# Two token blocks take turns in the first stage, with one order of loads and zero products in the gaps, in an attention kernel with two feed-forward layers

## The chip, the cores and the metric

The kernel runs on one core of one Trainium2 chip. The metric is the device time of one execution in microseconds (us). The median of three runs stands for a kernel.

## The reference: what is computed

Everything is float32, except the weights, which come as float64. First an attention in chunks of 32 queries, each of which sees its own 32 keys, 16 to the left, 8 to the right and 8 memory keys. Its output, 3072 tokens by 512, goes through two feed-forward layers of the same shape, one behind the other.

```python
        scores = scale * np.matmul(q_c, k_full.transpose(0, 1, 3, 2))
        scores = scores - np.max(scores, axis=-1, keepdims=True)
        a = np.exp(scores)
        a = a / (np.sum(a, axis=-1, keepdims=True) + 1e-09)
        out[:, :, c_start:c_end] = np.matmul(a, v_full)
...
    x = np.ascontiguousarray(attn_out.transpose(0, 2, 1, 3)).reshape(B * S, H * D)
...
    h = x @ w_in                                   # first layer, 512 -> 2048
    g = h * (1.0 / (1.0 + np.exp(-1.702 * h)))
    return (g @ w_out).astype(np.float32)          # 2048 -> 512
...
    h = x @ w_in                                   # second layer
    g = np.maximum(h, 0.0) + alpha * np.minimum(h, 0.0)
    return (g @ w_out).astype(np.float32)
```

## The kernel before

**Blocks and steps.** Each layer runs over six blocks of 512 tokens, and each block over 16 slices f of the hidden width, 128 columns each. A step is one block and one slice: `mm1` makes h in 12 products of 128x512 (TensorE; input and weight are each split into a high and a low part, and high-high, low-high and high-low are kept), `act1` and `split_g` make g and its two parts (ScalarE: tanh, cast; VectorE: two passes), and `mm2_t` adds 12 products into four accumulators y, which stay in four PSUM banks for the 16 steps of a block. The y products of a step are written behind the h products of the next (`LAG = 1`). After the 16th, `finish1` scales the four banks into SBUF, alternately on ScalarE and VectorE, and writes them to the DRAM tensor y1, which the second layer reads.

**Weights.** Piece s holds slice s of w_in and of w_out, 1 MB of float64 (`w_load`, two DMAs). It is turned into a high and a low float32 part: an absolute value on ScalarE (`w_abs`), four passes on VectorE (`w_bits`, L102 to L109), a cast on ScalarE (`w_high`, L120) and one more pass on VectorE (`w_low`, L125). The 16 pieces of the first layer are prepared while block 0 runs, since its step f needs piece f. `w_tick` hands out the next piece; the main loop asks for piece `W0 + WN*f/4`.

**Attention.** A group m is 128 tokens: scores (`a_scores`, tile sc), maximum and subtraction on VectorE, exp on ScalarE, sum and scaling on VectorE (into aspr or atpr), transposes on TensorE (pt) and copies on ScalarE (p), values (`a_pv`, tile xp), and a split into the high (ScalarE, L270) and low part (VectorE, L271) of x. A block needs four groups. Groups 0 to 3 run ahead of the first step (`NSTART = 4`), with two buffers for each of q, k and v (`SB = 2`); groups 4 to 7 run during block 0, and so on.

**Order.** A scheduler orders each engine's instructions at build time, except where `tc.keep_in_program_order` pins one; on the chip each engine goes through its list as it stands. All loads and stores are issued from one DMA queue on SyncE (SP), in order: an issue that waits for a free buffer holds the ones behind it.

Of the kernel before, what the change touches and what calls it, by code (L numbers as in the profile page):

```python
# [33 lines left out]
LAG = 1  # L34
NSTART = 4
WTICKS = (2, 3)
WAHEAD = 2
LEAD = 4
OPB = 3
W0 = 3  # L40
WN = 5
SB = 2
NWB = 4
NWARM = 28
# [4 lines left out]
@with_exitstack  # L49
def fused_kernel(ctx: ExitStack, tc: tile.TileContext, qs, ks, vs, ident, w_in1, w_out1, w_in2, w_out2, alpha, out):  # L50
    nc = tc.nc
# [78 lines left out]
    def w_tick(limit):  # L130
        s = wtick[0]
        if s >= limit + 1:
            return False
        if s - 1 in wst:
            w_low(s - 1)
        while wloaded[0] < limit and wloaded[0] <= s + (WAHEAD if wloaded[0] < BOOST else 1):
            w_load(wloaded[0])
            wloaded[0] += 1
        if s < limit:
            w_abs(s)  # L140
            w_bits(s)
# [59 lines left out]
    def a_max(m):  # L201
# [8 lines left out]
        mx = ap["pool"].tile([128, 2 * HP], F32, tag="mx", name=f"mx{m}")  # L210
        ex = ap["pool"].tile([128, 2 * HP, KW], F32, tag="p0", name=f"ex{m}", bufs=ap["pb"])
# [32 lines left out]
    def a_pcopy(m, g):  # L244
        s = st[m]
        s["p", g] = ap["pool"].tile([NK, HP, 128], F32, tag=f"p{g}", name=f"p{m}_{g}", bufs=ap["pb"] if g == 0 else None)
        nc.scalar.copy(s["p", g], s["pt", g])
# [88 lines left out]

    def mm2_t(p, y, gs, n, f):
        gh, gl = gs
        wh, wl = wt[p, f]
        for m in range(NKC):  # L340
            for i, (w, g) in enumerate(((wh, gh), (wh, gl), (wl, gh))):
                nc.tensor.matmul(  # L342
                    y[m][:, :n], w[:, 1, m * 128:(m + 1) * 128], g[:, :n],
                    start=(f == 0 and i == 0), stop=(f == NF - 1 and i == 2),
                )
# [10 lines left out]

    def finish1(y, t0, n):
# [32 lines left out]

    steps = []
    t0 = 0
    for j, n in enumerate(P1_BLOCKS):
        steps += [(1, j, t0, n, f) for f in range(NF)]
        t0 += n
    t0 = 0
    for j, n in enumerate(P2_BLOCKS):
        steps += [(2, j, t0, n, f) for f in range(NF)]
        t0 += n
    n1 = len(P1_BLOCKS)  # L400
    need = [done_tick(int(p1_start[j + 1]) // SQ - 1) for j in range(n1)]
    last1 = (n1 - 1) * NF

# [5 lines left out]

    t = ps2.tile([128, 128], F32, tag="h", name="warm")  # L410
    for i in range(NWARM):
        nc.tensor.matmul(t, warm, warm, start=True, stop=True)

    att_open("as", SB, 2)
# [6 lines left out]
    stags = ("a0", "a1", "y2", "y3")  # L421
    a_scores(0, stags[0])
    a_max(0)
    a_exp(0)
    for t in range(NSTART + 1):
        if t + 1 < NSTART:
            a_scores(t + 1, stags[(t + 1) % 4])
            a_load_v(t + 1)
        if t + 2 < NSTART:
            a_load(t + 2)  # L430
        if t < NSTART:
            a_norm(t)
            for g in range(2):
                a_trans(t, g, "h")
                a_pcopy(t, g)
        if t + 1 < NSTART:
            a_max(t + 1)
            a_exp(t + 1)
        if t < NSTART:
            a_pv(t, f"y{t % 2}")  # L440
            a_xcopy(t)
        if t in WTICKS:
            w_tick(NPC)
        if t == 1:
            nc.sync.dma_start(out=al_sb, in_=alpha.rearrange("(f p) -> p f", p=128))

    att.close()
    side["wpb"] = ctx.enter_context(tc.tile_pool(name="wpb", bufs=NWB))
    att_open("at", 1, 1)
    a_load(NSTART)  # L450
    a_load_v(NSTART)

    def do_mm2(i):
        p, j, t0, n, f = steps[i]
        if f == 0:
            ys[p, j] = [ps1.tile([128, DM], F32, tag=f"y{m}", name=f"y{m}") for m in range(NKC if p == 1 else n // 128)]
        (mm2_t if p == 1 else mm2_n)(p, ys[p, j], pend.pop(i), n, f)
        if f == NF - 1:
            (finish1 if p == 1 else finish2)(ys.pop((p, j)), t0, n)

    def attend(j, h):
        goal = need[j] + (need[j + 1] - need[j]) * min(1, h / (2 * NF - LEAD))
        while tick[0] < goal:
            a_tick()

    for i, (p, j, t0, n, f) in enumerate(steps):
        if i < NF:
            while wtick[0] < min(NPC + 1, W0 + (WN * f) // 4):
                w_tick(NPC)
        if i == last1:  # L470
            att.close()
# [6 lines left out]
        if i < last1:  # L478
            attend(j, 2 * f + 1)
        pend[i] = split_g(g, n, nc.vector)  # L480
        if i >= LAG:
            do_mm2(i - LAG)
        if i < last1:
            attend(j, 2 * f + 2)

# [56 lines left out]
```

## Time and profile before

| | |
|---|---|
| median of three runs | 1182.05 us (1181.15 to 1183.36) |
| the profiled execution | 1184.33 us, of which the span is 1182.6 us |
| TensorE (PE) busy | 1150.4 us, 97% of the span |
| VectorE (DVE) busy | 611.1 us, 52%; in 50 to 150 us it is 94.30 of 100 us |
| ScalarE (ACT) busy | 321.5 us, 27% |
| first h product | at 41.53 us |
| first block done (last y products) | about 160.9 us |
| second block done | about 262.4 us |

The shares are means over very different stages. In the first 160 us VectorE and the loads work much harder than later, and TensorE has its only gaps there; behind them TensorE is busy throughout. A matmul's end is modelled in the profile and overlaps the next, so the pitch from start to start is what it costs.

### The profile page before, as it was taken

To read this page: it belongs to the slowest core of one execution; us is meant where nothing else is said; L and a number is where in the kernel's file an instruction comes from. 1 tells how busy PE (TensorE), PEld (TensorE's weight loads), DVE (VectorE), ACT (ScalarE), POOL (GpSimd) and SP (SyncE) were. 2 spreads that over 40 slices of the span, in tenths; PEclk is the share of its full clock that TensorE was granted. 3 is DMA by queue.
4 is the path that set the end of the run, shared out by engine and by line. 5 is a ranking of instruction groups with operands and counts; after the bars stand their busy time and mean duration, and the time that the engine had idled before them with its cause. 6 is when DMAs were issued, how large, how long until landed. Compare 5 with 4: busy or idle time off the path is not lost.

```text
span 1182.6 us, 14925 instructions
## 1 busy us (share of the span) xinstructions
PE 1150.4 (97%) x6364; PEld 942.3 (80%) x6364; DVE 611.1 (52%) x871; ACT 321.5 (27%) x479; POOL 2.4 (0%) x10
## 2 busy tenths in 40 slices
PE   5799999999999999999999999999999999999998
PEld 5577788888888888888888788888888888888886
DVE  5899934343343434343699874434434434344433
ACT  2555433232323223223456321111111111111111
POOL 0000000000000000000000000000000000000000
PEclk8799999999999999999999999999999999999999
DMA  6964313121121212112544500200100000000000
GB/s 211 275 220 155 133 69 94 47 75 55 50 91 60 70 48 83 48 62 71 191 166 145 189 23 1 72 1 5 67 1 1 36 1 1 36 1 8 29 1 36
DMA packets 43578, 86.49 MB, mean 73 GB/s; under 512 B 5048, under 2 KB 21560, under 8 KB 43512
## 3 DMA queue, kind: packets, MB, share of 16 engines
q1 hardware_dynamic: 43512, 85.54, 21.9%
q8 instruction: 50, 0.82, 0.3%
q14 instruction: 16, 0.13, 0.0%
HBM read 72.95 MB, written 12.58 MB: 72 GB/s over the span
## 4 chain that ended last, share of the span: by engine, by line
PE 90%; DVE 4%; DMA 4%; ACT 1%; issue 1%; SPq 0%; ACTq 0%
PE h L312 42%; PE y L352 21%; PE y L342 21%; DMA wraw<-w_out 2%; PE xp L256 2%; PE sc L195 2%; PE pt L242 2%; DMA k<-ks 1%; DVE wtmp L109 1%; DVE wtmp L106 1%; DVE wlo L125 1%; DVE wtmp L102 0%; ACT wtmp L96 0%; DVE gl L334 0%; DVE atpr L232 0%
## 5 line engine op out<-in xcount | busy, mean ns | idle before, releaser
L312 PE MATMUL h<-x,whi 128*128 128x512 f32 x768 | 244.6, 398 | 2.7 <-ACT whi L120 1.9
L312 PE MATMUL h<-yx,whi 128*128 128x512 f32 x768 | 239.1, 390 | 1.1 <-DVE t L327 1.1
L333 ACT CAST gh<-t 128x512 fp32r<-128x512 f32 x192 | 119.2, 621 | 441.2 <-DVE t L327 372.5
L334 DVE TENSOR_TENSOR gl<-t,gh 128x512 fp32r<-128x512 f32 x192 | 132.4, 690 | 106.7 <-ACT gh L333 106.3
L326 DVE TENSOR_SCALAR t<-h,al_sb 128x512 f32<-128x512 f32 x96 | 72.0, 750 | 196.1 <-PE h L312 196.1
L312 PEld LDWEIGHTS h<-x,whi 128*128 128x128 f32 x768 | 143.8, 190 | 34.3 <-ACT whi L120 3.5
L312 PEld LDWEIGHTS h<-yx,whi 128*128 128x128 f32 x768 | 144.1, 188 | 32.4 <-DVE t L327 1.6
L321 DVE SCALAR_TENSOR_TENSOR t<-t,h 128x512 f32<-128x512 f32 x96 | 65.8, 685 | 184.9 <-ACT t L320 184.5
L312 PE MATMUL h<-x,wlo 128*128 128x512 f32 x384 | 152.1, 396 | 0.5 <-DVE wlo L125 0.5
L342 PE MATMUL y<-gl,whi 128*128 128x512 f32 x384 | 151.3, 394 | 0.4 <-DVE gl L334 0.4
L342 PE MATMUL y<-gh,wlo 128*128 128x512 f32 x384 | 150.7, 392 | 0.0
L312 PE MATMUL h<-yx,wlo 128*128 128x512 f32 x384 | 149.9, 390 | 0.0
L352 PE MATMUL y<-whi,gh 128*128 128x512 f32 x384 | 149.8, 390 | 0.0
L352 PE MATMUL y<-wlo,gh 128*128 128x512 f32 x384 | 149.7, 390 | 0.0
L352 PE MATMUL y<-whi,gl 128*128 128x512 f32 x384 | 142.6, 390 | 0.0
L342 PE MATMUL y<-gh,whi 128*128 128x512 f32 x384 | 128.1, 398 | 3.4 <-ACT gh L333 3.2
L320 ACT ACTIVATE t<-h 128x512 f32<-128x512 f32 x96 | 57.4, 598 | 185.5 <-PE h L312 185.4
L342 PEld LDWEIGHTS y<-gh,whi 128*128 128x128 f32 x384 | 70.7, 188 | 20.5 <-ACT gh L333 5.5
L312 PEld LDWEIGHTS h<-x,wlo 128*128 128x128 f32 x384 | 72.6, 189 | 16.7 <-DVE wlo L125 0.9
L342 PEld LDWEIGHTS y<-gl,whi 128*128 128x128 f32 x384 | 72.6, 189 | 16.3 <-DVE gl L334 0.8
L342 PEld LDWEIGHTS y<-gh,wlo 128*128 128x128 f32 x384 | 72.5, 189 | 15.6
L312 PEld LDWEIGHTS h<-yx,wlo 128*128 128x128 f32 x384 | 72.1, 188 | 15.5
(50 smaller groups left out, 916.0 us busy)
## 6 DMA issues: line engine op xcount, KB each, us to landing
wraw<-w_in SPq DMA_DIRECT2D x32, 512.0 KB
wraw<-w_out SPq DMA_DIRECT2D x32, 512.0 KB
q<-qs SPq DMA_DIRECT2D x24, 512.0 KB
k<-ks SPq DMA_DIRECT2D x24, 416.0 KB
v<-vs SPq DMA_DIRECT2D x24, 416.0 KB
y<-o SPq DMA_DIRECT2D x24, 256.0 KB
yraw<-y SPq DMA_DIRECT2D x6, 1024.0 KB
out<-o SPq DMA_DIRECT2D x24, 256.0 KB
```

Of the source, the lines that this page charges most:

```text
L106: nc.vector.scalar_tensor_tensor(out=a, in0=top, scalar=0xC0000000, in1=a, op0=ALU.bitwise_and, op1=ALU.bitwise_or)
L195: nc.tensor.matmul(sc[half[c], g, j, :], s["q"][:, g, j, c], s["k"][:, g, j, run[c]], start=True, stop=True,)
L242: nc.tensor.transpose(s["pt", g][:, j, :], s["pr"][:, g, j, :], id_sb)
L256: nc.tensor.matmul(x[half[z], g, j, :].rearrange("p (c q) -> p c q", c=2), s["v"][:, g, (2 * j + z) * D:(2 * j + z + 1) * D], p[:, j, z], ...
L312: nc.tensor.matmul(h[:, :n], w[:, 0, k * 128:(k + 1) * 128], x[:, z, k, :n], start=(i == 0), stop=(i == 3 * NKC - 1))
L320: nc.scalar.activation(out=t[:, :n], in_=h[:, :n], func=AF.Tanh, scale=1.702 / 2)
L321: nc.vector.scalar_tensor_tensor(out=t[:, :n], in0=t[:, :n], scalar=1.0, in1=h[:, :n], op0=ALU.add, op1=ALU.mult)
L326: nc.vector.tensor_scalar(out=t[:, :n], in0=h[:, :n], scalar1=0.0, scalar2=al_sb[:, f:f + 1], op0=ALU.min, op1=ALU.mult)
L333: nc.scalar.copy(gh[:, :n], g[:, :n])
L334: lo_eng.tensor_tensor(out=gl[:, :n], in0=g[:, :n], in1=gh[:, :n].bitcast(F32), op=ALU.subtract)
L342: nc.tensor.matmul(y[m][:, :n], w[:, 1, m * 128:(m + 1) * 128], g[:, :n], start=(f == 0 and i == 0), stop=(f == NF - 1 and i == 2),)
L352: nc.tensor.matmul(y[m], g[:, m * 128:(m + 1) * 128], w[:, 1, :], start=(f == 0 and i == 0), stop=(f == NF - 1 and i == 2),)
```

## The change

Blocks 0 and 1 are cut into four phases: slices 0 to 5 of block 0, the same of block 1, then slices 6 to 15 of block 0 and of block 1. The weight pieces 0 to 5 serve 12 steps before piece 6 is needed. At the end of the first two phases ScalarE writes half-finished y sums to y1 (all four banks, the DMAs issued from ScalarE's own queue), and at the end of the other two they are loaded back (`load_part`) and added by VectorE. Eight groups instead of four run in the part that is written out by hand: four ahead of the first step, four during the first four steps. Their q is stored without zeros (half the bytes), and GpSimd writes the zeros. There are five buffers for q and k and six for v. The loads alternate between groups and weight pieces; alpha goes behind the weights. The absolute value on ScalarE of pieces 1 to 6 keeps its place in the program. Products of a zero tile (128x128, bfloat16), 24 at a time and in seven places (168), stand in TensorE's list between the parts of groups 0 to 3.

```diff
@@
+NFIRST = 4
+NSTART = 8
+HEAD = 6
+PINNED = 7
+NKEEP = 24
+WTICKS = (0, 2)
...
+SB = 5
+NWB = 8
...
-        nc.scalar.activation(out=a.bitcast(F32), in_=wst[s][0][:, :, 1].bitcast(F32), func=AF.Abs)
+        i = nc.scalar.activation(out=a.bitcast(F32), in_=wst[s][0][:, :, 1].bitcast(F32), func=AF.Abs)
+        if 0 < s < PINNED:
+            tc.keep_in_program_order(i)
...
     def a_load(m):
+        if m < NSTART:
+            q = ap["pool"].tile([128, 2, 2, CHUNK, 2 * HP], F32, tag="q", name=f"q{m}")
+            for z in range(2):
+                nc.gpsimd.memset(q[half[z], :, 1 - z], 0.0)
+                nc.sync.dma_start(out=q[half[z], :, z].rearrange("p g q i -> p g (q i)"), in_=q0[m, half[z]])
...
+    def finish1(y, j, last):
+        t0, n = int(p1_start[j]), P1_BLOCKS[j]
+        if not last:
+            for m in range(NKC):
+                o = op.tile([128, TBM], F32, tag="o", name="o")
+                nc.scalar.mul(o[:, :n], y[m][:, :n], 0.5)
+                nc.scalar.dma_start(out=y1[m, :, t0:t0 + n], in_=o[:, :n])
+            return
+        part = parts.pop(j, None)
         for m in range(NKC):
             o = op.tile([128, TBM], F32, tag="o", name="o")
-            if m % 2:
+            if part is not None:
+                nc.vector.scalar_tensor_tensor(
+                    out=o[:, :n], in0=y[m][:, :n], scalar=0.5, in1=part[:, m, :n], op0=ALU.mult, op1=ALU.add
+                )
+            elif m % 2:
...
+    phases = [(0, 0, HEAD), (1, 0, HEAD), (0, HEAD, NF), (1, HEAD, NF)]
+    phases += [(j, 0, NF) for j in range(2, len(P1_BLOCKS))]
...
+    def keep_warm(n):
+        t = ps1.tile([128, 128], F32, tag="a1", name="warm")
+        for i in range(n):
+            tc.keep_in_program_order(nc.tensor.matmul(t, warm, warm, start=True, stop=True))
...
     a_load(0)
     a_load_v(0)
+    nc.sync.dma_start(out=id_sb, in_=ident)
     w_load(0)
-    nc.sync.dma_start(out=id_sb, in_=ident)
-    a_load(1)
-    wloaded[0] = 1
+    for m in range(1, NFIRST):
+        a_load(m)
+        a_load_v(m)
+    w_load(1)
...
+    for t in range(NFIRST):
+        if t + 1 < NFIRST:
+            a_scores(t + 1, stags[t + 1])
+            keep_warm(NKEEP)
+        a_norm(t)
...
+        a_load(t + NFIRST)
+        a_load_v(t + NFIRST)
+        if t < 3:
+            w_load(wloaded[0])
+            wloaded[0] += 1
...
+            while wtick[0] < min(NPC + 1, 3 + i if i < HEAD else 3 + HEAD + (3 * (i - HEAD)) // 4):
                 w_tick(NPC)
...
+        if p == 1 and f == 0 and j == 2:
+            tc.keep_in_program_order(nc.sync.dma_start(out=al_sb, in_=alpha.rearrange("(f p) -> p f", p=128)))
+        if p == 1 and f == NF - 2 and ph == 2:
+            a_load(NSTART)
+            a_load_v(NSTART)
```

The lists themselves show it at three places. The number behind a name tells tiles apart, the one behind wraw, whi and wlo is the weight piece. From the third step of block 2 on (on SyncE from group 10's q on) the lists of before and of the change are the same.

First place: SyncE's queue of DMA issues at the start, from the second group's v (before) and q (change) on. Before:

```order
L186 DMA v_184<-vs 104x1024
L445 DMA al_sb<-alpha 128x16x1
L179 DMA q_186<-qs 128x1024
L181 DMA k_188<-ks 128x832
L179 DMA q_254<-qs 128x1024
L181 DMA k_256<-ks 128x832
L186 DMA v_252<-vs 104x1024
L186 DMA v_320<-vs 104x1024
L85 DMA wraw_1_366<-w_in 128x4x256
```

And with the change:

```order
L188 DMA q_143<-q 64x2x256 x2
L191 DMA k_148<-ks 128x832
L202 DMA v_150<-vs 104x1024
L188 DMA q_152<-q 64x2x256 x2
L191 DMA k_157<-ks 128x832
L202 DMA v_159<-vs 104x1024
L188 DMA q_161<-q 64x2x256 x2
L191 DMA k_166<-ks 128x832
L202 DMA v_168<-vs 104x1024
L87 DMA wraw_1_170<-w_in 128x4x256
```

Alpha is gone from between the groups, and piece 1 stands directly behind group 3, with no wait for a buffer ahead of it.

Second place: VectorE's list around the last weight piece of the first layer (wlo_15). Before, where h_1365 is the h of the 15th step:

```order
L106 SCALAR_TENSOR_TENSOR wtmp<-wraw_15_1102,wtmp 128x1024
L334 TENSOR_TENSOR gl<-t,gh 128x512
L109 SCALAR_TENSOR_TENSOR wtmp<-wraw_15_1102,wtmp 128x1024
L271 TENSOR_TENSOR x_672<-xp_1324,x_672 128x2x4x64
L213 TENSOR_REDUCE mx_1360<-sc_1343 128x8
L125 TENSOR_TENSOR wlo_15_1211<-wtmp,whi_15_1210 128x1024
L214 TENSOR_TENSOR ex_1361<-sc_1343,mx_1360 128x512
L321 SCALAR_TENSOR_TENSOR t<-t,h_1365 128x512
```

With the change, where h_1590 and h_1632 are the h of the 16th and the 17th step:

```order
L110 SCALAR_TENSOR_TENSOR wtmp<-wraw_15_1542,wtmp 128x1024
L337 SCALAR_TENSOR_TENSOR t<-t,h_1590 128x512
L350 TENSOR_TENSOR gl<-t,gh 128x512
L113 SCALAR_TENSOR_TENSOR wtmp<-wraw_15_1542,wtmp 128x1024
L350 TENSOR_TENSOR gl<-t,gh 128x512
L337 SCALAR_TENSOR_TENSOR t<-t,h_1632 128x512
L129 TENSOR_TENSOR wlo_15_1630<-wtmp,whi_15_1629 128x1024
L350 TENSOR_TENSOR gl<-t,gh 128x512
```

The last piece is ready behind the 17th step's work on h; before, ahead of the 15th's.

Third place: ScalarE's list at the end of the first phase (y_869 to y_872 are the four banks of block 0, h_1191 and h_1235 the first two steps of block 1), with the change; before, a block's banks have two rows on ScalarE and two on VectorE.

```order
L124 CAST whi_6_1098<-wtmp 128x1024
L124 CAST whi_7_1143<-wtmp 128x1024
L386 ACTIVATE o<-y_869 128x512
L386 ACTIVATE o<-y_870 128x512
L386 ACTIVATE o<-y_871 128x512
L98 ACTIVATE wtmp<-wraw_8_1089 128x1024
L387 DMA y_83<-o 128x512 x3
L98 ACTIVATE wtmp<-wraw_9_1134 128x1024
L336 ACTIVATE t<-h_1191 128x512
L336 ACTIVATE t<-h_1235 128x512
L349 CAST gh<-t 128x512
L386 ACTIVATE o<-y_872 128x512
```

The fourth bank is emptied behind the first h work of the next phase.

## Rows read from the trace of the kernel before

**Rows 1.** The page's first line: the span of the profiled execution.
```profile
span 1182.6 us, 14925 instructions
```

**Rows 2.** Stages: start:end, length, busy us (count) by engine, clock, DMA share, GB/s.
```profile
core 0: us, PE busy (x) PEld busy (x) DVE busy (x) ACT busy (x) POOL busy (x), PEclk, DMA share, GB/s
...
14.00:16.00 2.00, 2.00 (x29) 1.63 (x29) 1.93 (x3) 1.17 (x2) 0.00 (x0) 1.00 0.80 32
24.00:30.00 6.00, 5.75 (x72) 5.15 (x72) 4.18 (x8) 1.76 (x4) 0.00 (x0) 0.53 0.01 3
...
36.00:50.00 14.00, 9.41 (x54) 6.71 (x54) 11.51 (x14) 7.41 (x9) 0.00 (x0) 0.51 1.01 313
44.00:50.00 6.00, 6.00 (x15) 4.29 (x17) 5.82 (x7) 2.66 (x3) 0.00 (x0) 0.50 1.01 293
50.00:150.00 100.00, 95.01 (x655) 75.10 (x656) 94.30 (x130) 52.36 (x72) 0.00 (x0) 0.98 0.54 180
41.50:160.90 119.40, 112.70 (x718) 88.60 (x719) 108.04 (x149) 59.58 (x81) 0.00 (x0) 0.95 0.53 173
160.90:262.40 101.50, 101.50 (x673) 83.10 (x673) 41.00 (x70) 29.73 (x51) 0.00 (x0) 1.00 0.21 65
...
651.60:1171.40 519.80, 518.65 (x2279) 427.17 (x2277) 238.14 (x326) 82.44 (x120) 0.00 (x0) 1.00 0.07 26
```

**Rows 3.** SyncE's issues at the start, in order: start, length of the issue.
```profile
5.86 0.38 SPq L445 DMA_DIRECT2D al_sb<-alpha  x1
7.98 6.94 SPq L179 DMA_DIRECT2D q<-qs  x1
...
17.42 12.73 SPq L186 DMA_DIRECT2D v<-vs  x2
```

**Rows 4.** TensorE in order, first 45 us: start, length, [idle before <- who ended it].
```profile
1.00 3.17 PE L412 MATMUL warm<-warm 128*128 128x128 bf16 x28 [1.00 <-DVE warm L408]
5.98 1.98 PE L195 MATMUL sc<-k,q 128*64 128x64 f32 x32 [1.81 <-DMA k<-ks]
...
24.03 1.98 PE L195 MATMUL sc<-k,q 128*64 128x64 f32 x32 [1.36 <-DMA k<-ks]
...
30.92 1.05 PE L242 MATMUL pt<-id_sb,aspr 128*104 128x128 f32 x8 [1.14 <-DVE aspr L232]
32.26 0.69 PE L256 MATMUL xp<-p,v 104*64 104x64 f32 x16 [0.29 <-ACT p L247]
...
44.00 1.22 PE L312 MATMUL h<-x,whi 128*128 128x512 f32 x2 [1.67 <-ACT whi L120]
```

**Rows 5.** VectorE in order, first group and first weight piece.
```profile
8.18 0.69 DVE L213 TENSOR_REDUCE mx<-sc 128x8 f32<-128x512 f32 x1
...
10.29 0.69 DVE L227 TENSOR_REDUCE sm<-ex 128x8 f32<-128x512 f32 x1 [0.69 <-ACT ex L221]
...
12.87 0.69 DVE L102 TENSOR_SCALAR wtmp<-wtmp 128x1024 f32<-128x1024 f32 x1
```

**Rows 6.** ScalarE in order, second group: a copy of transposed weights, an exp.
```profile
27.07 0.59 ACT L247 COPY p<-pt 104x512 f32<-104x512 f32 x1 [8.16 <-PE pt L242]
27.55 0.63 ACT L221 ACTIVATE ex<-ex 128x512 f32<-128x512 f32 x1
```

**Rows 7.** VectorE in order, back to back, and the last weight piece.
```profile
57.32 1.22 DVE L125 TENSOR_TENSOR wlo<-wtmp,whi 128x1024 fp32r<-128x1024 f32 x1
58.46 0.68 DVE L227 TENSOR_REDUCE sm<-ex 128x8 f32<-128x512 f32 x1
59.05 0.68 DVE L321 SCALAR_TENSOR_TENSOR t<-t,h 128x512 f32<-128x512 f32 x1
...
146.71 1.22 DVE L125 TENSOR_TENSOR wlo<-wtmp,whi 128x1024 fp32r<-128x1024 f32 x1
```

**Rows 8.** Emptying the y banks, whole run: length least/median/most in ns.
```profile
L363 DVE TENSOR_SCALAR o<-y x12: 680/684/692, 160.2 to 657.0; 128x512 f32<-128x512 f32 x12
L361 ACT ACTIVATE o<-y x12: 597/600/601, 160.7 to 658.2; 128x512 f32<-128x512 f32 x12
```

More of the change, by code (lines that the diff above doesn't have):

```diff
@@ L49, in fused_kernel @@
 @with_exitstack
-def fused_kernel(ctx: ExitStack, tc: tile.TileContext, qs, ks, vs, ident, w_in1, w_out1, w_in2, w_out2, alpha, out):
+def fused_kernel(ctx: ExitStack, tc: tile.TileContext, q0, qs, ks, vs, ident, w_in1, w_out1, w_in2, w_out2, alpha, out):
     nc = tc.nc
@@ L142, in w_tick @@
             w_high(s)
+            if s < HEAD + 2:
+                w_low(s)
         wtick[0] += 1
@@ L343, in mm2_t @@
                     y[m][:, :n], w[:, 1, m * 128:(m + 1) * 128], g[:, :n],
-                    start=(f == 0 and i == 0), stop=(f == NF - 1 and i == 2),
+                    start=(f == fa and i == 0), stop=(f == fb - 1 and i == 2),
                 )
@@ L408, in fused_kernel @@
     nc.vector.memset(warm, 0.0)
[L410 to L414, printed above, removed]
+    def keep_warm(n):
+        t = ps1.tile([128, 128], F32, tag="a1", name="warm")
+        for i in range(n):
+            tc.keep_in_program_order(nc.tensor.matmul(t, warm, warm, start=True, stop=True))
+    keep_warm(NWARM)
+    att_open("as", SB, 2, 3)
     a_load(0)
     a_load_v(0)
+    nc.sync.dma_start(out=id_sb, in_=ident)
@@ L437, in fused_kernel @@
             a_max(t + 1)
             a_exp(t + 1)
-        if t < NSTART:
-            a_pv(t, f"y{t % 2}")
-            a_xcopy(t)
+        a_pv(t, f"y{t % 2}")
+        a_xcopy(t)
+        if t + 1 < NFIRST:
+            keep_warm(NKEEP)
         if t in WTICKS:
             w_tick(NPC)
[L444 to L449, printed above, removed]
@@ L450, in fused_kernel, with steady @@
-    a_load(NSTART)
-    a_load_v(NSTART)
-    def do_mm2(i):
-        p, j, t0, n, f = steps[i]
+        a_load(t + NFIRST)
[3 more added lines that the diff above has]
+            wloaded[0] += 1
+    a_scores(NFIRST, "a1")
+    a_max(NFIRST)
+    a_exp(NFIRST)
+    def steady():
+        att.close()
+        side["wpb"] = ctx.enter_context(tc.tile_pool(name="wpb", bufs=NWB))
+        att_open("at", 1, 1, 1)
+    def do_mm2(i):
+        p, ph, j, t0, n, f = steps[i]
+        if p == 1:
+            _, fa, fb = phases[ph]
+            if f == fa:
+                ys[ph] = [ps1.tile([128, TBM], F32, tag=f"y{m}", name=f"y{m}") for m in range(NKC)]
+            mm2_t(p, ys[ph], pend.pop(i), n, f, fa, fb)
+            if f == fb - 1:
+                finish1(ys.pop(ph), j, fb == NF)
+            return
@@ L463, in attend @@
+    def attend(ph, f, half_step):
+        _, a, b = phases[ph]
+        span = 2 * (b - a) - (LEAD if b - a > HEAD else 1)
+        goal = need[ph] + (need[ph + 1] - need[ph]) * min(1, (2 * (f - a) + half_step) / span)
         while tick[0] < goal:
             a_tick()
-    for i, (p, j, t0, n, f) in enumerate(steps):
-        if i < NF:
-            while wtick[0] < min(NPC + 1, W0 + (WN * f) // 4):
+    for i, (p, ph, j, t0, n, f) in enumerate(steps):
+        if NSTART - NFIRST <= i < last1:
+            while wtick[0] < min(NPC + 1, 3 + i if i < HEAD else 3 + HEAD + (3 * (i - HEAD)) // 4):
@@ L469, in fused_kernel @@
                 w_tick(NPC)
+        now = NFIRST + i if i < NSTART - NFIRST else None
+        if now is not None:
+            while wtick[0] < min(3 + i, NF - 2 - NWB):
+                w_tick(NPC)
+            a_norm(now)
+            if now + 1 < NSTART:
+                a_scores(now + 1, "a1")
+                a_max(now + 1)
+                a_exp(now + 1)
+            for q in range(2):
+                a_trans(now, q, "a0")
+                a_pcopy(now, q)
+            a_pv(now, "a0")
+            a_xcopy(now)
+            if now + 1 == NSTART:
+                steady()
```

92 lines of the change are left out of this document (45 added, 47 removed).

## The prediction

> **What bounds the kernel now.** I read the stages first, then the waits inside them. From 160.9 to 262.4 us, the second block, TensorE is busy for all of 101.50 us at full clock, VectorE for 41.00; the second layer looks the same, and its 95 steps in 519.80 us make 5.47 us a step, or 0.228 us for each of the 24 products [rows 2]. So behind the first block the kernel is a stream of products that nothing holds up. What can be won lies ahead of 160.9 us. A block with the attention of the next costs 101.5 us at full speed; the first product that is followed by others starts at 44.00 [rows 4], and block 0 ends at 160.9. The account of before is thus 44.0 + 101.5 + 15.4 us of loss inside block 0.
>
> Two things make these numbers. Up to 44 us it is a chain of loads and small work: SyncE holds an issue for 6.94 us and another for 12.73 us, from 17.42 to 30.15, because a buffer of q or v isn't free, and the weight pieces 1 to 3 stand behind it [rows 3]; from 24 to 30 us the DMA engines are used to 1% [rows 2]. From 44 on it is VectorE: between 50 and 150 us it is busy for 94.30 of 100 us, TensorE for 95.01, and only here [rows 2]. A step needs one weight piece, two VectorE passes for g and a share of a group. The last weight pass starts at 146.71 [rows 7], and behind it there is no more loss. Besides, the first products run at half clock: 15 in the 6.00 us from 44 to 50, with the clock at 0.50 [rows 2]; at 0.228 us they would take 3.4.
>
> **The change, part by part.** The lists from the third step of block 2 on are the same, so all of the difference arises ahead of the end of block 1.
>
> *Start.* I add VectorE's list up to the low part of group 3's x. A group has maximum and subtraction (0.69 each), 2.58 us from the start of the sum at 10.29 to the next work at 12.87, and 0.69 for the low part, by the same row [rows 5]: 4.65, times four 18.6. Piece 0 takes two passes of 0.69 and three of 1.22 [rows 5, 7], 5.0; ahead of that last low part the new list has also the four bit passes of piece 1 (3.8), the first of piece 2 (0.7) and maximum, subtraction and sum of group 4 (2.1). Together 30.2. It starts about 7.3, when the scores of group 0 are done: 5.98 + 1.98 before [rows 4], less 0.7 for the halved q. Then what it waits for: group 0's exp, 0.69 [rows 5]; and in two later rounds the next exp, which stands on ScalarE behind the two copies of the transposes: 1.05 + 2 x 0.59 + 0.63 = 2.86 [rows 4, 6], against 0.69 of subtraction as cover, so 2.2 twice; and one burst of 24 zero products on that path. The trace has such products only at 3.17 us for 28, 113 ns each [rows 4]; at twice the clock, an estimate from that, 57 ns, so 24 take 1.4 to 2.7 us; I take 1.4, as TensorE is then working for most of the time. Sum 7.3 + 30.2 + 0.7 + 4.4 + 1.4 = 44.0. **The start gains nothing**; the loads do come earlier (alpha's scattered 2.00 us at 32 GB/s [rows 2] and both holds are gone), but the chain through three engines takes their place. It has, though, done 1.4 us more of VectorE's work than before at 44.0 (group 4's three passes, less one pass of piece 2). Bounds: 41, if each of those waits is half; 48 with the bursts at half speed.
>
> *Until the last weight pass.* Before: 44.0 to 147.9, 103.9 us. The same passes are due, and by the two lists five more passes for g (0.60 each at the pitch of back-to-back rows, as 58.46 to 59.05 [rows 7]) and most of group 8 (2.9), less the 1.4 that are done: 4.5, at 94.3% busy 4.8 us. So the last weight pass ends at 152.7. But TensorE stands further on by then: two more sets of h products and two thirds of a set of y (32 products, 7.3 us), and 1.7 us of group 8. It may also run ahead by up to a step, as the last piece isn't due for five more steps; of 0 to 5.5 I take 2.5. That is 11.5 further at 4.8 later: **6.7 us gained**.
>
> *Seams.* There are two more ends of a phase. Four banks on ScalarE take 4 x 0.60 [rows 8] where before two engines shared them, and the fourth, for want of a third free output buffer, goes behind the next tanh and two weight passes of ScalarE. Its cover is the 12 to 24 h products (2.7 to 5.5 us) that TensorE does before it needs that bank. The adding back is 4 x 0.68 [rows 8] on VectorE in a row, under some 13 products, 3.0 us. Uncovered they'd cost 2.4 each; I take 0.5 each, **1.0 us lost**. The loads of the half sums (1 MB each) fall where the DMA engines have room (share 0.21 [rows 2]).
>
> *Group 8.* Its loads stand on SyncE behind those of piece 11, which wait for the buffer of piece 7, freed just ahead of the end of phase 1. Two MB at 313 GB/s [rows 2] are 6.3 us and about 2 more of issue and latency; its scores stand on TensorE behind two steps of h of phase 2, 5.5 us. TensorE goes by its list, as at 24.03, when scores waited 1.36 us for k [rows 4] with everything behind them. So 0 to 4 lost; I take **1.5**. [...]
>
> GpSimd's zeros for q lie ahead of the loads' landing or beside other work (it is otherwise idle); the pinned absolute values wait only for loads that are long there; alpha's new place has idle DMA engines. If that cover is gone, a group's zeros are two memsets on its path, under 1 us each by their size.
>
> Sum: 0 - 6.7 + 1.0 + 1.5 = -4.2. The profiled execution took 1184.33 us (span 1182.6 [rows 1] and 1.7 around it), so 1180.1 for its like; it lies 2.3 above the median of 1182.05, and I predict for the median **1178**.
>
> **The rivals.**
> - *VectorE isn't the bound any more* (chance 0.14). Six weight pieces serve twelve steps, and TensorE runs from 44.0 without loss, with the scores of groups 4 and 5 (2.2) done. End of block 1 at 44.0 - 2.2 + 203.0 + 2.5 = 247.3 against 262.4: 15 us gained, **1167**. Against it: up to the end of phase 1 four whole groups and eight pieces are due, some 48 us of VectorE for 43 of TensorE.
> - *No change* (0.18). The slack goes: the run-ahead is 0, group 8 costs 3 and the seams 1.5 together. 4.2 - 2.5 - 1.5 - 0.5 is about 0: **1182**, from 1179.7 to 1184.4.
> - *Slower* (0.18). TensorE stays at half clock through the start, as it did from 24 to 30 us at 5.75 of 6 busy (0.53) and from 36 to 50 (0.51) [rows 2]. Then each burst costs 1.3 more, four of which aren't covered (5.3), and scores, transposes and values of three groups 0.9 each (8): about 12 later, with the lists fixed behind it: **1190**. It decides from 5 us on. For it: 28 zero products right ahead of them did not make the first scores at 5.98 any faster (1.98 us) [rows 4]. Against it: in my chain TensorE is busy for five sixths of the time between 10 and 44. [...]
> - *As forecast* (0.50): 1174 to 1181.
>
> **How the numbers follow.** A measurement of this kernel tells about 0.2%, 2.4 us, from no change. The forecast's own range lies on the faster side up to a few hundredths; so faster 0.48 + 0.14 = 0.62, within 0.2% 0.02 + 0.15 = 0.17, and slower 0.18 + 0.03 = 0.21, the last from the upper edge of no change. The range reaches from the first rival at 1167 to 1186, which leaves out the worse part of the slower case and some of the best, under 2 in 10.
>
> **What would show it.** Right: the first run of h products near 44 us at full clock; VectorE over 90% busy to about 150 us with TensorE's gaps in phase 1 ended by VectorE and ScalarE; the last first-layer weight pass near 153 with 17 sets of h done; the last y products of block 1 at 258; short gaps at the seams and one at group 8's scores, ended by k. From there the same length as before, 920 us. Wrong: if the half-clock products of the start go on (slower), if the first phase has no gaps (1167), or if the stage behind block 1 differs at all, which none of this explains.

## The result and the profile after

The changed kernel takes 1188.6 us in the median of four runs (1186.46 to 1190.78), against 1181.65 for the kernel before on the same chip: a ratio of 1.0053, 95% interval 1.0033 to 1.0074. It is slower by 6 to 7 us, where 4 less had been forecast. The profiled execution took 1186.46 us, the fastest of its four; a second profile, of a run of 1192.14 us, comes with the experiments. One execution of e8 there, of 4079.72 us, is left out of its ratio.

The windows of the changed kernel, which answer to [rows 2] (busy time by engine, clock, DMA share, GB/s):

```profile
2.00:16.00 14.00, 7.19 (x80) 6.60 (x78) 6.31 (x11) 1.78 (x3) 7.23 (x15) 0.83 1.00 256
16.00:30.00 14.00, 12.27 (x178) 11.68 (x179) 7.60 (x12) 3.23 (x5) 2.07 (x4) 0.80 1.05 254
30.00:50.00 20.00, 17.88 (x293) 16.05 (x292) 14.74 (x27) 9.73 (x15) 0.00 (x0) 1.00 1.02 251
49.50:98.50 49.00, 47.45 (x368) 37.55 (x369) 47.62 (x71) 26.32 (x38) 0.00 (x0) 1.00 0.62 179
98.50:160.00 61.50, 60.26 (x330) 48.46 (x329) 56.13 (x70) 34.76 (x49) 0.00 (x0) 1.00 0.54 183
160.00:262.80 102.80, 102.80 (x629) 83.14 (x629) 42.50 (x72) 27.66 (x47) 0.00 (x0) 1.00 0.22 69
```

Two things stand out. The granted clock is 1.00 from 30 us on, where before it was 0.51 from 36 to 50 us. And in the whole start the DMA engines are never free (share 1.00 to 1.05), yet they move only 251 to 256 GB/s; before, the same share moved 313 from 36 to 50 us [rows 2]. TensorE in order, as in [rows 4]:

```profile
6.30 2.20 PE L211 MATMUL sc<-k,q 128*64 128x64 f32 x32 [2.14 <-DMA k<-ks]
8.43 2.74 PE L453 MATMUL warm<-warm 128*128 128x128 bf16 x24
15.85 2.20 PE L211 MATMUL sc<-k,q 128*64 128x64 f32 x32 [4.67 <-DMA k<-ks]
17.98 2.74 PE L453 MATMUL warm<-warm 128*128 128x128 bf16 x24
20.51 1.52 PE L258 MATMUL pt<-id_sb,aspr 128*104 128x128 f32 x8
21.96 2.15 PE L211 MATMUL sc<-k,q 128*64 128x64 f32 x32
25.84 1.51 PE L211 MATMUL sc<-k,q 128*64 128x64 f32 x21 [1.73 <-DMA k<-ks]
...
28.34 1.51 PE L453 MATMUL warm<-warm 128*128 128x128 bf16 x24
29.78 0.94 PE L211 MATMUL sc<-k,q 128*64 128x64 f32 x10
...
41.46 2.15 PE L211 MATMUL sc<-k,q 128*64 128x64 f32 x32
...
49.53 0.82 PE L328 MATMUL h<-x,whi 128*128 128x512 f32 x2 [1.08 <-ACT whi L124]
...
105.32 1.15 PE L211 MATMUL sc<-k,q 128*64 128x64 f32 x32 [1.24 <-DMA k<-ks]
```

The run of h products starts at 49.53, not at 44. The scores of three groups (0, 1 and 3) wait for k. A score set takes 2.15 us at full clock (at 41.46, granted 1.00) where group 8's at 105.32, whose q has the old layout, takes 1.15 at the same clock. The chain of waits tells how late k comes (start, length, what):

```profile
5.88 9.72 DMA k<-ks
15.60 0.02 issue
15.62 9.98 DMA k<-ks
25.59 0.25 issue
25.84 1.50 PE sc L211 x21
```

Group 3's k is issued the moment group 1's k lands. In SyncE's list these are the 18th and the 10th load: the 18th waits until the 10th is there, so eight are under way. The issues around it keep the same distance: the 14th (at 10.30) waits 0.3 us for the 6th, the 15th (12.31) 1.6 for the 7th, the 19th (17.43) 1.5 for the 11th. No issue up to 30 us waits for GpSimd: from the first issue on all of SyncE's waits, 1.6 us at the longest, are for loads. VectorE, at the places of [rows 5, 7 and 8]:

```profile
18.09 0.69 DVE L229 TENSOR_REDUCE mx<-sc 128x8 f32<-128x512 f32 x1 [1.86 <-PE sc L211]
...
24.16 0.69 DVE L229 TENSOR_REDUCE mx<-sc 128x8 f32<-128x512 f32 x1 [1.91 <-PE sc L211]
...
29.07 0.69 DVE L287 TENSOR_TENSOR x<-xp,x 128x512 fp32r<-128x512 f32 x1 [1.77 <-ACT x L286]
30.75 0.69 DVE L229 TENSOR_REDUCE mx<-sc 128x8 f32<-128x512 f32 x1 [0.99 <-PE sc L211]
...
34.33 0.69 DVE L243 TENSOR_REDUCE sm<-ex 128x8 f32<-128x512 f32 x1 [2.29 <-ACT ex L237]
...
49.12 0.68 DVE L287 TENSOR_TENSOR x<-xp,x 128x512 fp32r<-128x512 f32 x1
...
157.83 1.22 DVE L129 TENSOR_TENSOR wlo<-wtmp,whi 128x1024 fp32r<-128x1024 f32 x1
...
262.77 1.88 DVE L393 SCALAR_TENSOR_TENSOR o<-y,part 128x512 f32<-128x512 f32 x3
```

The adding back of block 1's half sums starts at 262.77, where before its first bank was emptied at 261.67: most of the late start has been made good by then. ScalarE's first bank of the fifth and of the sixth block in the changed kernel:

```profile
568.06 0.60 ACT L397 ACTIVATE o<-y 128x512 f32<-128x512 f32 x1 [0.27 <-PE y L358]
...
656.40 0.59 ACT L397 ACTIVATE o<-y 128x512 f32<-128x512 f32 x1
```

Before, these stand at 567.98 and 655.38. So at 568 us the two profiles are level: 5.5 us of late start against 5.4 us won behind it. Then, where both lists are the same, 1 us is lost, and from 671 us on a constant 1.8.

### The profile page after: what moved, and what is told of

Read it like the earlier page. It is cut to its first block, busy times and chain, and to the rows that moved or that the text cites. A ratio compares the mean times of both kernels' runs of the same rounds, so it can differ in the third digit from the quotient of the medians.

```text
span 1184.5 us, 15314 instructions
## 1 busy us (share of the span) xinstructions
PE 1162.3 (98%) x6532; PEld 954.2 (81%) x6532; DVE 612.7 (52%) x875; ACT 322.2 (27%) x483; POOL 10.7 (1%) x26
## 4 chain that ended last, share of the span: by engine, by line
PE 88%; DVE 7%; DMA 3%; SPq 1%; issue 1%; ACT 0%; ACTq 0%
PE h L328 41%; PE y L368 21%; PE y L358 20%; DMA k<-ks 2%; PE xp L272 2%; PE sc L211 2%; PE pt L258 1%; DVE wtmp L113 1%; DVE wtmp L110 1%; DVE wlo L129 1%; PE warm L453 1%; DVE wtmp L106 1%; DVE gl L350 1%; DMA wraw<-w_out 1%; DVE wtmp L107 0%
## 5 line engine op out<-in xcount | busy, mean ns | idle before, releaser
L368 PEld LDWEIGHTS y<-whi,gh 128*128 128x128 f32 x384 | 72.1, 188 | 15.4
```

What stands on the lines that cost most here:

```text
L368: nc.tensor.matmul(y[m], g[:, m * 128:(m + 1) * 128], w[:, 1, :], start=(f == 0 and i == 0), stop=(f == NF - 1 and i == 2),)
```

## The experiments

All are edits of the changed kernel unless said otherwise. Ratios are to the kernel before, timed beside each; 0.001 is 1.2 us. The last three columns are of one profile of each run, and two profiles of one kernel differ there by up to 2.8 us. "h" is the start of the unbroken run of h products, "block 4" (the fifth block) the time at which ScalarE empties its first bank of y, "block 5" the time from there to the same point of block 5: 16 steps without attention, at 5.47 us [rows 2] 87.5 us without loss.

| run | ratio | 95% interval | h | block 4 | block 5 |
|---|---|---|---|---|---|
| kernel before, two profiles (e15) | 1.0004 (e15) | 0.9996 to 1.0013 | 44.00, 44.37 | 568.0, 565.5 | 87.4, 87.4 |
| changed, two profiles (e7) | 1.0053, 1.0052 | 1.0033 to 1.0074, 1.0038 to 1.0065 | 49.53, 51.34 | 568.1, 570.9 | 88.3, 90.1 |
| e1 full strided q | 0.9986 | 0.9977 to 0.9995 | 44.79 | 564.4 | 88.3 |
| e2 dense q | 0.9983 | 0.9971 to 0.9995 | 46.59 | 564.8 | 88.8 |
| e3 no zero products | 1.0062 | 1.0047 to 1.0077 | 50.66 | 570.8 | 87.4 |
| e4 no turns | 1.0093 | 1.0079 to 1.0106 | 51.57 | 574.2 | 90.5 |
| e5 half q, long runs | 1.0046 | 1.0029 to 1.0062 | 47.00 | 565.8 | 90.5 |
| e6 full q and zeros | 1.0049 | 1.0034 to 1.0064 | 48.67 | 568.2 | 87.9 |
| e8 dense, piece 0 late | 1.0021 | 1.0012 to 1.0030 | 48.66 | 567.6 | 87.9 |
| e9 full q, two halves of partitions | 1.0126 | 1.0097 to 1.0156 | 58.46 | 579.6 | 89.2 |
| e10 half q from ScalarE | 1.0067 | 1.0053 to 1.0081 | 52.77 | 571.1 | 88.4 |
| e11 dense, v from ScalarE | 1.0119 | 1.0104 to 1.0135 | 59.72 | 578.7 | 87.9 |
| e12 half q, staged | 1.0022 | 1.0012 to 1.0031 | 49.25 | 568.6 | 87.8 |
| e13 full q, two issues by columns | 1.0019 | 1.0008 to 1.0030 | 48.54 | 568.2 | 87.9 |
| e14 dense, idle zeros | 0.9973 | 0.9961 to 0.9984 | 42.43 | 560.6 | 88.8 |
| e16 19 zero products | 1.0026 | 1.0014 to 1.0037 | 46.71 | 568.0 | 87.4 |
| e17 dense, 19 zero products | 0.9986 | 0.9972 to 1.0000 | 44.67 | 566.3 | 87.4 |
| e18 dense, v behind | 0.9970 | 0.9961 to 0.9980 | 43.82 | 563.7 | 87.6 |

**The parts of the change: e1 to e4.** The trace suggested the scores' stride of 8 floats as the first theory; the rivals were the loads, the zero products and the turns. In e1 q0 holds the zeros too, in the same strided order; e2 loads q of all groups from qs, as the kernel before does. e4 also asks for weight piece `3 + i` at each step i.

```diff
@@ e1 @@
-            for z in range(2):
-                nc.gpsimd.memset(q[half[z], :, 1 - z], 0.0)
-                nc.sync.dma_start(out=q[half[z], :, z].rearrange("p g q i -> p g (q i)"), in_=q0[m, half[z]])
+            nc.sync.dma_start(out=q.rearrange("p g q i -> p (g q i)"), in_=q0[m])
@@ e3 @@
-NKEEP = 24
+NKEEP = 0
@@ e4 @@
-    phases = [(0, 0, HEAD), (1, 0, HEAD), (0, HEAD, NF), (1, HEAD, NF)]
-    phases += [(j, 0, NF) for j in range(2, len(P1_BLOCKS))]
+    phases = [(j, 0, NF) for j in range(len(P1_BLOCKS))]
```

> The changed kernel, but q of groups 0 to 7 is loaded with its zeros (512 KB a group in long runs, no zeros from GpSimd), still in the order that makes the scores read it with a stride of 8 floats. Theory A (the stride is what makes the start late): scores stay at 2.10 to 2.20 us, the first run of h products stays near 49.5 us, and the time at 1188.6, within 1.5. Theory B (short runs and GpSimd's zeros make it late): h near 45 to 46 and 1184 to 1185. Theory C (the loads bind by their bytes): 1 MB more up to group 3 at 252 GB/s is 4 us, so h near 53 and 1192.

> The changed kernel, but q of groups 0 to 7 is loaded as before: with its zeros and in the order that the scores read without a stride. It differs from the run with full strided q in the stride alone. Theory A (stride): scores back at 1.10 us at full clock, the two that stand just ahead of h (groups 4 and 5) give 2.1 us and one more on the chain 1, so h 3 us earlier than with full strided q, and 3 us less time: about 1185.5. Theory C (loads): the same time as with full strided q, within 1 us, since the chain waits for k.

> The changed kernel without the seven bursts of 24 zero products between the groups (the 28 at the very start stay). Theory D (zeros cost): the bursts at 17.98 (2.7 us), 28.34 and 30.65 (1.45 each) stand ahead of transposes that are due; part of it is lost in the wait for k at 25.84, so h 2.9 to 5.6 us earlier and 1183 to 1186, with the clock at 1.00 from 22 us on or soon after. Theory E (zeros hold the clock): the scores, transposes and first h products fall back to 0.5 of the clock, as before the change, and the time is 1190 to 1194.

> The changed kernel with its start, loads and zeros, but blocks 0 and 1 one behind the other, without half sums; a weight piece for each step of block 0. Theory F (the turns gain what was forecast of them, the start loses it): block 0 loses some 11 us to VectorE again where the changed kernel lost 5.6 in all, so about 1194. Theory G (the turns gain nothing, since their seams and group 8's wait eat it): 1188.6 within 1.5.

e1 was 1181.35 us, below the kernel before and some 8 us off the changed kernel, though it loads twice the bytes of q: theory B, beyond its own figure of 1184 to 1185. It takes away the short runs, GpSimd's zeros, the second issue and the 64 partitions all at once. e2, without the stride, is no further (the intervals overlap). **The stride theory falls**: 1 us more for each of eight score sets is real, but it isn't what makes the start late, and the time of e2 doesn't show it. The windows of e1 show what is new:

```profile
2.00:16.00 14.00, 8.61 (x101) 7.79 (x100) 6.74 (x12) 2.95 (x5) 1.02 (x3) 0.85 1.00 325
16.00:30.00 14.00, 14.00 (x234) 13.12 (x233) 9.02 (x14) 4.08 (x7) 0.00 (x0) 0.91 1.05 332
```

At the same DMA share the loads run at 325 and 332 GB/s instead of 256 and 254. e4 answers to theory F: without the turns 0.0040 more, 4.7 us. e3 lies between its theories, close to E; the windows, clock in the third place from the end, are

```profile
2.00:16.00 14.00, 4.92 (x63) 4.53 (x61) 6.17 (x11) 1.78 (x3) 7.23 (x15) 0.70 0.98 257
16.00:30.00 14.00, 9.57 (x132) 8.75 (x129) 7.68 (x13) 3.23 (x5) 2.08 (x4) 0.69 1.04 252
30.00:50.00 20.00, 12.57 (x185) 11.15 (x185) 14.53 (x25) 9.21 (x15) 0.00 (x0) 0.74 1.01 266
```

Without the zero products the clock is down to 0.74 where it was 1.00, and h starts at 50.66, so what the zeros take from the chain and what the full clock gives back about cancel. The whole moves by no more than the intervals, also because this run gets back in block 5 (87.4) what the changed kernel loses there; e16 below shows why.

**What of q's load is slow: e5 to e9, e13, e14.** Four things come with the halved q: runs of 1 KB, zeros by GpSimd, two issues a group, and 64 partitions an issue. e5 orders the tile so that an issue writes 2 KB in a row. e6, e9 and e13 are edits of e1; e8 is e2 with `w_load(0)` behind the loads of groups 1 to 3, and e14 is e2 with the memsets into a tile of their own. e7 is the changed kernel again.

```diff
@@ e5 @@
-            q = ap["pool"].tile([128, 2, 2, CHUNK, 2 * HP], F32, tag="q", name=f"q{m}")
+            q = ap["pool"].tile([128, 2, CHUNK, 2, 2 * HP], F32, tag="q", name=f"q{m}")
@@ e6, ahead of the load @@
+            for z in range(2):
+                nc.gpsimd.memset(q[half[z], :, CHUNK * (1 - z):CHUNK * (2 - z)], 0.0)
@@ e9, in place of the load @@
+            for z in range(2):
+                nc.sync.dma_start(out=q[half[z]].rearrange("p g q i -> p (g q i)"), in_=q0[m, half[z]])
@@ e13, in place of the load @@
+            for g in range(2):
+                nc.sync.dma_start(out=q[:, g].rearrange("p q i -> p (q i)"), in_=q0[m, :, 512 * g:512 * (g + 1)])
```

> The changed kernel with q still stored without zeros and with GpSimd's zeros, but laid out so that one load writes 2 KB in a row in each partition (half as many packets) instead of two runs of 1 KB; the scores' stride becomes 16 floats. Theory P (the short runs cost the DMA engines): the loads get ahead of those of the run with full strided q by up to 1 MB, h near 44 to 46, and about 1181. Theory M (GpSimd's zeros, for which the issues of q wait, and the two issues in place of one): nothing changes, h near 49.5 and within 1.5 of the changed kernel run beside it.

> The run with full strided q, with GpSimd's two memsets of a group written ahead of its load again (they are overwritten). It puts back the wait of the load for GpSimd, not the short runs and not the second issue. Theory M: h back near 49.5 and 5 to 7 us more than the full strided run's ratio of 0.9986, so 1.004 to 1.005. Theory P: as the full strided run, 0.9986 within 0.0010.

> The changed kernel itself once more, as the yardstick for the runs beside it: 1.0053 of the kernel before, within 0.0015. If most of what is left unexplained of its profile (it is only 0.1 us behind the kernel before at 568 us, but the median is 6.9 behind) is the run-to-run part, this profile will stand at another place there.

> The run with dense q, with weight piece 0 issued behind the loads of group 3 instead of ahead of those of group 1. Theory L (the start waits for its loads in their order: k of group 3 ended 3.44 us of idling at 25.94): 1 MB less ahead of it at about 300 GB/s, k of group 3 some 3.3 us earlier, h 2 to 3 us earlier and 1178 for a kernel before of 1183 (ratio 0.996). Theory V (VectorE's work sets the start): the five passes of piece 0 lose their place between 12 and 20 us, and it is 2 to 4 us later (ratio 1.000 to 1.002).

> The run with full strided q, whose q load of 512 KB is cut into two issues of 64 partitions each, as the changed kernel's halves are; no zeros from GpSimd. Theory Q (SyncE keeps at most eight loads under way: by the changed kernel's list the 18th issue, k of group 3 at 15.62, starts as the tenth, k of group 1, lands; two small issues in place of one long one take two of the eight places, so the loads behind them are issued later): about as slow as the changed kernel, ratio 1.004 to 1.006. Theory M (GpSimd's zeros are what costs): as the full strided run, 0.9986 within 0.0015. Halfway would leave part to either.

> The run with full strided q, its load cut into two issues by columns, each 256 KB into all 128 partitions. Against the run cut by partition halves (1.0126) only the partitions that an issue writes differ. Theory H (an issue into 64 partitions is slow and slows the loads around it: there k's packets took 262 ns in the median against 133 with whole q): near the full strided run, 0.998 to 1.001. Theory Q (two issues take two of eight places): 1.010 to 1.013 again.

> The run with dense q, with GpSimd's sixteen memsets at their place in the program, but into a tile that nobody reads. Theory M (GpSimd's work itself disturbs the start): 1.003 to 1.006. Otherwise: as the dense run, 0.9983 within 0.0015.

e5's profile has h at 47.00 and its loads run at 266 and 282 GB/s (256 and 254 in the changed kernel), but its time isn't told from the changed kernel's: theory P's 1181 isn't borne out, though the short runs may have a part in the loads. e6 looked like theory M, but doesn't test it: the scheduler put the first q behind weight piece 0, and the scores of group 0 waited for it:

```profile
11.17 2.20 PE L211 MATMUL sc<-k,q 128*64 128x64 f32 x32 [7.01 <-DMA q<-q]
```

e14 is the clean test: as many memsets at the same place cost nothing (0.9973). Nor do the issues of q wait for the zeros in the changed kernel's own trace (their waits up to 30 us, 1.4 us at the longest, are for loads), and e9, with no zeros at all, is slower still. **Theory M falls.** e9 and e13 load the same bytes in as many issues and differ only in how q is cut (by partitions into rows of 4 KB, by columns into rows of 2 KB). The windows of e9, and then of e13:

```profile
2.00:16.00 14.00, 7.28 (x80) 6.69 (x78) 3.93 (x8) 1.03 (x3) 1.02 (x3) 1.00 0.99 231
16.00:30.00 14.00, 9.97 (x157) 9.25 (x156) 9.44 (x14) 3.99 (x6) 0.00 (x0) 0.76 1.04 197
```

```profile
2.00:16.00 14.00, 6.89 (x81) 6.38 (x79) 4.66 (x10) 1.77 (x3) 1.02 (x3) 0.82 0.97 281
16.00:30.00 14.00, 13.86 (x196) 12.63 (x194) 9.94 (x14) 3.89 (x6) 0.00 (x0) 0.81 1.05 254
```

Cut by partitions the loads fall to 197 GB/s, and the time is 1.0126 against 1.0019: 12.6 us between the two cuts (theory H). Two issues by columns in place of one cost the 3.9 us between e1 and e13. That they do so by their two of eight places (theory Q) is argued, not shown: the DMA share is 0.97 to 1.05 in e13 too, so the engines don't lack loads, while the packets of k (3328 bytes, 2 to 30 us) take 206 ns in the median, against 133 in e1 and 260 in e9. In e12 below, with rows of 2 KB in one issue, they take 134, so the shorter rows alone don't do it.

e8 went against theory L: it was 4.5 us slower than e2, though its second scores started at 11.69 us (e2: 13.88). Weight pieces 0 and 1 are now issued one behind the other, 11.57 to 17.2 us, and their passes on VectorE fall together ahead of h; TensorE then waits 4.25 and 2.94 us for VectorE's scaling of groups 3 and 4 (theory V).

**Other ways to load: e10 to e12, e18.** e10 issues the changed kernel's q loads by `nc.scalar.dma_start`; e11 is e2 with the v loads of groups 0 to 7 issued so. e12 loads q's half in one piece into a staging tile t:

```diff
@@ e12 @@
+            nc.sync.dma_start(out=t.rearrange("p i q -> p (i q)"), in_=q0[m].rearrange("p g i -> p (g i)"))
...
+            for z in range(2):
+                nc.gpsimd.tensor_copy(q[half[z], :, z], t[half[z]])
@@ e18, from e2 @@
-    for m in range(1, NFIRST):
-        a_load(m)
-        a_load_v(m)
+    a_load(1)
+    for m in range(2, NFIRST):
+        a_load(m)
+        a_load_v(m - 1)
+    a_load_v(NFIRST - 1)
```

> The changed kernel with its halved q, GpSimd's zeros and two issues a group, but these issues stand in ScalarE's queue instead of SyncE's. Theory Q: k, v and the weights come earlier, as their places in SyncE's queue are free, and with 1 MB less up to group 3 than in the full strided run: h at 43 to 45 and a ratio of 0.996 to 0.999. Theory M: as the changed kernel, 1.004 to 1.006, since the zeros are as before.

> The run with dense q, with the v loads of groups 0 to 7 issued from ScalarE's queue instead of SyncE's. Theory Q: more bytes under way, k of group 3 earlier than 25.94 (about 22) and the ratio below that of the dense run (0.9983), 0.995 to 0.997. If the DMA engines are full anyway with dense q (rival), the ratio stays at 0.998 to 0.999.

> The changed kernel with q's half in one load of 256 KB into 128 partitions of a staging tile, from where GpSimd copies the two halves between its zeros (dense order, no stride). Theory H: the loads run at the rate of the dense run or better with 1 MB less up to group 3, h at 42 to 45, ratio 0.994 to 0.998. Rival: GpSimd's copies (two of 64x512 a group, in order behind each other and behind the landing) come into the chain, 1 to 2 us a group, and the ratio is 0.999 to 1.003.

> The run with dense q (24 zero products), with the v loads of groups 1 to 3 behind the next group's q and k. If the start waits for k (3.44 us at 25.94 in one profile of the dense run, none in that with idle zeros): k of group 3 some 2 us earlier, ratio 0.996 to 0.997. If not, v is late for group 1's values instead: 0.998 to 1.000.

e10 and e11 both missed, for a reason that no theory had. The issues stand in ScalarE's list, and ScalarE waits in them (e10's ScalarE):

```profile
0.75 10.92 ACTq L188 DMA_DIRECT2D q<-q  x8
11.69 1.28 ACT L237 ACT_TABLE_LOAD   x1 [11.69 <-DMA q<-q]
...
16.17 10.04 ACTq L188 DMA_DIRECT2D q<-q  x5
```

Its exp of group 0 came at 12.99 instead of 10.18. So they say nothing for theory M against theory Q. e12 gave the rival's figure: loads at 319 and 289 GB/s in the two windows, but h at 49.25, as GpSimd's copies come in order behind each landing and its scores waited 3.93 and 2.50 us for them. e18 was 0.9970, the lowest of all with e14, and faster than both kernels; from e2 (0.9983) the intervals don't tell it.

**The stage behind: e15 to e17.** The changed kernel lost time also where both lists are the same. e15 is the kernel before once more; e16 has `NKEEP = 19` in place of 24, and e17 the same with dense q.

> The kernel before itself, for a second profile of it. If the 1.7 us that the changed kernel's profile loses between 568 and 671 us are the run's and not the program's, this profile can differ there from the first (568.0, 655.4, 744.3 for the marks at the end of blocks 4 and 5 and of the second layer's first block) by as much; if they are the program's, it agrees within 0.5 us. Ratio 1.000 within 0.001.

> The changed kernel with 19 instead of 24 zero products in each of the seven bursts: 69 instructions fewer in TensorE's list, so that its code packet, which fell into the weight load between 628 and 634 us, comes some 8 us later, between two loads. Theory K (the code packet delays that load): from the end of block 4 to that of block 5, 87.4 us as in the kernel before (88.3 and 90.1 in the changed kernel), and to the next mark 88.9 (89.7 and 90.6); ratio 1.002 to 1.004. Rival: the stage varies from run to run without it; 88 to 90 again and 1.0053 within 0.0012.

> The same with dense q. If Theory K holds, its stage takes 87.4 where the dense runs took 88.7 to 88.8, and its ratio is 0.996 to 0.997; otherwise 0.9978 within 0.0012.

Two profiles of the kernel before agree there to 0.1 us, so the loss is the program's. In the changed kernel one weight load, issued at 628.00, is late (SyncE, then ScalarE, then the DMA queues from 631 to 632 us: packets, MB, share):

```profile
628.00 0.51 SPq L91 DMA_DIRECT2D wraw<-w_out  x1
...
634.16 1.13 ACT L98 ACTIVATE wtmp<-wraw 128x1024 f32<-128x1024 f32 x1 [4.51 <-DMA wraw<-w_out]
...
q8 instruction: 1, 0.02, 6.0%
```

6.16 us from issue to use, against 632.42 - 627.78 = 4.64 before. It is the tenth load of a w_out slice in block 5. In e16 the tenth takes 632.11 - 627.51 = 4.60 us. The seventh and the eleventh are

```profile
607.85 0.51 SPq L91 DMA_DIRECT2D wraw<-w_out  x1
...
633.73 0.51 SPq L91 DMA_DIRECT2D wraw<-w_out  x1
```

```profile
613.93 1.15 ACT L98 ACTIVATE wtmp<-wraw 128x1024 f32<-128x1024 f32 x1 [2.75 <-DMA wraw<-w_out]
...
638.39 1.16 ACT L98 ACTIVATE wtmp<-wraw 128x1024 f32<-128x1024 f32 x1 [0.80 <-DMA wraw<-w_out]
```

The eleventh takes 4.66 us again, the seventh 6.08; block 5 takes 87.4 us, in e17 too. **That the count of zero products alone moves this stage by 0.9 to 2.7 us is shown.** e16's ratio fell by 0.0027 as theory K has it; e17's did not, and its profile reaches block 4 at 566.3, later than e2's (564.8) and e14's (560.6).

That a packet of code (16 KB on the DMA queue q8, one every 24 to 31 us in this stage) is the cause is argued, and the late load does not account for the loss. A packet that comes 0.8 to 3.9 us behind the issue of the tenth load goes with a load of 5.99 to 7.39 us (both profiles of the changed kernel, e4, e5, e9, e10). At 3.8 to 4.2 us in nine others the load was not late (among them e1, e2 and e14, which lose 0.9 to 1.4 us in block 5 all the same). In e16 the packet came 2.9 us behind the issue of the seventh load, which was late, and block 5 lost nothing. What does go with the loss in all twenty profiles is the place of the packets: one comes within the tenth load in each of the fifteen in which block 5 takes 87.6 us or more, and in none of the five with 87.4.

## Why the prediction was wrong, point by point

- **The step that failed is "The start gains nothing", with its sum of 44.0.** h came at 49.53 and 51.34. VectorE, from its first work to the end of the low part of group 3's x, in the changed kernel:

```profile
8.58:49.80 41.22, 32.69 (x490) 30.10 (x488) 28.46 (x49) 14.72 (x22) 3.26 (x7) 0.88 1.04 256
```

It starts at 8.58 instead of 7.3, works for 28.46 us instead of 30.2, and waits 41.22 - 28.46 = 12.8 instead of 0.7 + 4.4 + 1.4 = 6.5, which is 6.3 more. The two waits for exp were about right (2.29 and 1.70 for 2.2 each). "Less 0.7 for the halved q" should have been 0.5 more, as the first scores came at 6.30 and took 2.20 us. The sum has no wait for a load at all. VectorE waited 1.86 us for the scores of group 1, whose k came late, and 1.77 us for x of group 0, whose values stand on TensorE behind the scores of group 3 and their wait for k. It waited 1.91 and 0.99 us for the scores of groups 2 and 3, which stand behind a burst of zero products each. These four make 6.5 us. And "the loads do come earlier" was not worked out. Before, the scores of groups 1 and 2 start at

```profile
14.79 1.65 PE L195 MATMUL sc<-k,q 128*64 128x64 f32 x32
...
20.69 1.98 PE L195 MATMUL sc<-k,q 128*64 128x64 f32 x32 [3.31 <-DMA k<-ks]
```

and those of groups 0 and 3 at 5.98 and 24.03 [rows 4]. In the changed kernel all four start later, at 6.30, 15.85, 21.96 and 25.84. No rate was set for the loads of the start; the only one in the text is 313 GB/s [rows 2], of loads into 128 partitions, and the start moved 251 to 256. e1, which takes the halved q away with all that comes with it, starts at 44.79, near the forecast, and is 8 us faster.
- *Zero products*: 1.4 on the path was too little. That the clock would be full wherever TensorE works most of the time was the author's estimate, and no run shows it: from 17.98 to 20.72 us TensorE was busy for all of 2.74 us at 0.50. The first two of the seven bursts ran at half clock (2.74 us each, at a granted clock of 0.50), the later ones at 63 ns a product (1.00), and by the waits above two of them held up scores. They do hold the clock from 30 to 50 us (1.00, against 0.74 without them in e3). So the rival *Slower* came true in those two bursts, but not in the rest of its mechanism, though 1188.6 lies near its 1190: the cause was another.
- *Until the last weight pass, seams, group 8*: -6.7 + 1.0 + 1.5 = -4.2. From h to block 4's mark it was 524.0 us before and 518.5 with the change, 521.1 and 519.5 in the second profiles: -5.5 and -1.6, in the mean -3.5. The last weight pass ended at 157.83 + 1.22 = 159.05 instead of 152.7, and 5.5 of that is the lateness of the start. TensorE shows no gap at the seams (of its four waits from 50 to 262 us, 1.24 at the longest, none is for a bank of y), so that 1.0 was too much. Group 8 waited 1.24 us, ended by k (1.5 had been taken). e4 confirms the turns: 4.7 us, of which its profile shows 3.2 to 4.2 between h and block 4.
- *VectorE not the bound* (1167): no. VectorE is busy for 47.62 of 49 us in the first phases (TensorE for 47.45), and block 1 ends at about 262.8; less the 5.5 of late start that is 257.3, near the forecast's 258 and not at this rival's 247.3.
- *"From there the same length as before"*: wrong by 1.7 us in the first profile, and in the second by (90.1 - 87.4) for block 5 and 1.7 for the block behind it. The text named this as what would make it wrong. The lists are the same, but not the times at which the code packets come; that these are the cause is not shown.

In sum, by the two pairs of profiles: up to block 4 the changed kernel is 569.5 - 566.8 = 2.7 us later (6.2 of late start, less 3.5), and behind it 1.7 to 4.4. That makes 4.4 to 7.1, with 6.2 to 6.3 measured (0.0052 and 0.0053). Not settled are how the two issues, the 64 partitions and the short runs share the loss when q is halved, since e9 and e13 carry the whole q, and why e17 starts later than e14.

## What to carry to other kernels

Price a load by the partitions it writes and by the issues it is cut into, not by its bytes alone: here one issue of 512 KB into 128 partitions beat two of 128 KB into 64 by 8 us, as the loads around them came later; and the whole q in two issues cost 3.9 us more than in one when cut by columns (e13, e1), and 12.6 more again when cut by partitions (e9). When a start has a DMA share of 1.0, put every load of its chain into the sum. And when two versions differ behind the point from which their lists agree, look for what still differs, here the times at which code is loaded (a packet between 631 and 632 us in the changed kernel, between 637 and 638 in e16), before you call it noise.

## What the runs showed of the hardware

- From 2 to 30 us, at a DMA share of 0.97 to 1.05, a mix with q's loads of 256 KB into 64 partitions moves 197 to 231 GB/s (e9); with q cut by columns 254 to 281 (e13), with q whole 325 to 332 (e1).
- Eight loads of SyncE's queue are under way at a time: the 18th issue (15.62 us) waits for the 10th load (15.60), and the ones around it keep the distance.
- A q that is read with a stride of 8 floats makes 32 score products take 2.15 us (at 41.46, changed kernel) in place of 1.15 (group 8's at 105.32), at a granted clock of 1.00 in both.
- Zero products keep the granted clock at 1.00 through a stage (30 to 50 us, changed kernel) in which it is 0.74 without them (e3); in the other runs with 24 of them it lies between 0.83 and 1.00 there (in e18 a score set takes 1.98 us at 41.91, behind a wait of 3.60 us for k, and 1.15 at 51.88). The same product takes 114 ns at a granted clock of 0.50 and 63 ns at 1.00 (changed kernel, at 17.98 and 28.34).
- 70 instructions fewer at the start of TensorE's list (35 zero products and their weight loads, e16) changed the time of a stage 600 us later by 0.9 to 2.7 us.
